# Attention, MoE and FFN in one kernel: the next expert's weights split by slices of 1024, in another order

## The chip, the cores and the metric

The kernel runs on one core of a Trainium2 chip. The metric is the device time of one execution in microseconds. TensorE (PE in the profile) multiplies matrices; its weight loads have a row of their own (PEld). VectorE (DVE), ScalarE (ACT) and GpSimd (POOL) compute elementwise. SyncE (SP) issues DMA transfers; POOL issues the indirect ones, which gather or scatter rows.

## What is computed

```python
attn_out = _attn_ref(**attn_kwargs)                 # 2 x 8 heads x 768 x 64, window 128, 4 sinks
x = np.ascontiguousarray(attn_out.transpose(0, 2, 1, 3)).reshape(B * S, H * D)   # 1536 x 512
x = _moe_ref(x=x, **moe_kwargs)                     # 8 experts, top 1
return _moe2_ref(x=x, **moe2_kwargs)                # (relu(x @ w_in) ** 2) @ w_out, d_ff 2048

# in _moe_ref, disp holds each expert's tokens (at most 384)
h = np.maximum(np.einsum('ecd,edf->ecf', disp, w1), 0.0)    # w1: 512 x 1024 for each expert
y = np.einsum('ecf,efd->ecd', h, w2)                        # w2: 1024 x 512 for each expert
out[i] = gate_w[i] * y[expert_idx[i], pos[i]]
```

## The kernel before

The kernel has three stages: attention with routing, the experts (MoE), and the last FFN. The change lies in the MoE stage.

**Precision.** Every fp32 matrix product is made of three matmuls on a high and a low part: `a_h b_h + a_h b_l + a_l b_h`. A tile is split by two instructions: ScalarE copies it to `h` in the type fp32r, and VectorE subtracts `h` from it into `l`. The weights of an expert are 4 MB, eight slices of 128x1024: four of `w1`, four of `w2`. `Weights.split` (L141) splits half a slice, 512 columns, at a time, so an expert has 16 such splits, each with a copy on ScalarE (L144) and a subtraction on VectorE (L145).

**Raw weights.** `fetch` (L135) loads a slice from memory into a ring of six raw slots. `freed` (L119) is called when a slice's second half is split; it lets `pull` issue the next load, which goes on SP's queue and waits for VectorE's subtraction of the slice that held the slot, six slices back.

**Order of the work.** The order of each engine's instructions is that of the Python code (a manual schedule). For expert `e` the loop calls `body(e, 0, ...)` for its first block of 128 tokens, then `more` for further blocks; these are behind an `If` on the expert's count, read at run time, so after the first block every engine passes a conditional branch and, later, the place where its two ways join. `body` splits the weights of expert `e + 1` between its own steps, and the table `HEAVY` says how many splits go into each gap. The steps are:

- `g1(0)`: 12 matmuls for the first half of h; then a gap, `relu(0)` (ScalarE, `hs`), `g1(1, [0, 1])`, a gap;
- `tr(0)`: TensorE transposes the first half of `hs`, ScalarE casts it to `hTh` (L913), VectorE subtracts into `hTl` (L914); `g1(1, [2, 3])`, a gap, `relu(1)`;
- `g2([0, 1])`: 6 matmuls into y; a gap, `tr(1)`, `g2([2, 3])`;
- point 2: `pre` transposes x for the same expert's second block (`xT1`) and the next expert's first (`xT0`); ScalarE casts them (L872), VectorE subtracts (L873) and computes the gates (L877, L878);
- a gap, `g2([4, 5])`, `g2([6, 7])`, a gap;
- `ys` (L956): VectorE scales y out of PSUM; POOL scatters it to `yd` (L957); then the splits that are left.

Each engine takes its queue in order, so a step behind a split waits for it. The last expert, 7, has no next one; it stages pieces of the FFN's weights (`piece_stage`, L174 to L189) instead, by the table `LAST`. At the end of its first block `load_y` (L1001) has SP load rows of `yd` (L1009), which waits for the scatters of the experts before, and TensorE transposes them to `x2T` (L1015).

Of the kernel before, what the change touches and what calls it, by code (L numbers as in the profile page):

```python
# [8 lines left out]
F32 = mybir.dt.float32  # L9
# [9 lines left out]
NOBODY = 8192  # L19
NWARM0 = 10  # L20

HEAVY = (3, 1, 2, 2, 0, 4)
LIGHT = (1, 1, 1, 1, 1, 1)
LAST = (0, 0, 1, 0, 1, 1)
NWARM = 2
PTACT = (0, 2)
SPOOL = ()
SDVE = ()
FILL = {0: 4, 1: 4, 2: 2, 3: 2}


# [1 line left out]
def kernel(  # L33
# [15 lines left out]
    nc = tc.nc  # L49
# [36 lines left out]
    def ps(tag, name):  # L86
        banks[tag].append(banks[tag].pop(0))
        return psum.tile([P, 512], F32, tag=f"b{banks[tag][-1]}", name=name)
# [18 lines left out]
    def pull(n):  # L107

        nonlocal held
        while n and stream and held + stream[0][0] <= NRAW:  # L110
            held += stream[0][0]
            n -= 1
            stream.pop(0)[1]()

    def freed(n=1):
        nonlocal held
        held -= n
        if eager:
            pull(NRAW)  # L119

    class Weights:
# [19 lines left out]
        def split(self, n, eng=None, hi=None):  # L141
            i, sl = n // 2, slice(n % 2 * 512, n % 2 * 512 + 512)
            t = self.raw[i]
            (hi or nc.scalar.copy)(self.h[i][:, sl], t[:, sl])  # L144
            (eng or nc.vector).tensor_sub(self.l[i][:, sl], t[:, sl], self.h[i].bitcast(F32)[:, sl])  # L145
            if n % 2:
                freed()

# [68 lines left out]
    W = {0: Weights(0, wx, "x"), 1: Weights(1, None, "y")}  # L219
# [629 lines left out]
    def gate_at(e, b):  # L849
        return gate[2 + b % 2 if b else e % 2]  # L850

    def load_x(e, b):
        if e >= E or b >= nblk:
            return
        nc.gpsimd.indirect_dma_start(
            out=x_at(e, b), out_offset=None, in_=xd[:, :], in_offset=bass.IndirectOffsetOnAxis(ap=src[:, b, e : e + 1], axis=0),
            bounds_check=NTOK - 1, oob_is_err=False,
        )

    def pre(e, b):  # L860
        if e >= E or b >= nblk:
            return
        p_ = ps("bg", "xT")
        for c in range(KD):
            nc.tensor.transpose(p_[:, c * P : (c + 1) * P], x_at(e, b)[:, c * P : (c + 1) * P], ident)
        pre_split(e, b, p_)
        pre_gate(e, b, x_at(e, b)[:, DM:])
# [12 lines left out]
    def body(e, b, splits, plan, also):  # L880
        xh, xl = xT[e, b]
        wts = W[e]
        splits = list(splits)

        def sp(n):
            for _ in range(n):
                if splits:
                    splits.pop(0)()

        hs = mp.tile([P, F], F32, tag="hs", name="hs", bufs=1)  # L890
        hp = [None, None]

        def g1(half, ks):
            if ks[0] == 0:
                hp[half] = ps("s" if half or b else "iv", "h")
            for kk in ks:
                r = slice(half * 512, half * 512 + 512)
                for m, (a, bb) in enumerate(((xh, wts.h), (xh, wts.l), (xl, wts.h))):
                    nc.tensor.matmul(hp[half], a[:, kk, :], bb[kk][:, r], start=(kk == 0 and m == 0), stop=(kk == KD - 1 and m == 2))

        def relu(half):
            nc.scalar.activation(hs[:, half * 512 : half * 512 + 512], hp[half], AF.Relu)

        hT = [None, None]

        def tr(half):
            p_ = ps("pt", "hT")
            for c in range(4):
                o0 = half * 512 + c * P
                nc.tensor.transpose(p_[:, c * P : (c + 1) * P], hs[:, o0 : o0 + P], ident)  # L910
            h_ = mp.tile([P, 512], F32R, tag="hTh", name="hTh", bufs=2)
            l_ = mp.tile([P, 512], F32R, tag="hTl", name="hTl", bufs=2)
            nc.scalar.copy(h_, p_)  # L913
            nc.vector.tensor_sub(l_, p_, h_.bitcast(F32))  # L914
            hT[half] = (h_, l_)

        y = ps("ot", "y")

        def g2(fs):
            for f in fs:  # L920
                h_, l_ = (x[:, (f % 4) * P : (f % 4 + 1) * P] for x in hT[f // 4])
                wh, wl = wts.h[KD + f // 2], wts.l[KD + f // 2]
                r = slice((f % 2) * 512, (f % 2) * 512 + 512)
                for m, (a, bb) in enumerate(((h_, wh), (h_, wl), (l_, wh))):
                    nc.tensor.matmul(y, a, bb[:, r], start=(f == 0 and m == 0), stop=(f == NF - 1 and m == 2))

        def point(i):
            for f in also.get(i, ()):
                f()

        plan = iter(plan)
        g1(0, [0, 1, 2, 3])
        sp(next(plan))
        relu(0)
        g1(1, [0, 1])
        sp(next(plan))
        tr(0)
        g1(1, [2, 3])
        sp(next(plan))
        relu(1)  # L940
        point(0)
        g2([0, 1])
        sp(next(plan))
        tr(1)
        point(1)
        g2([2, 3])
        point(2)
        sp(next(plan))
        g2([4, 5])
        point(3)  # L950
        g2([6, 7])
        point(4)
        sp(next(plan))
        y_ = mp.tile([P, DM + 1], F32, tag="ys", name="ys", bufs=2)
        nc.gpsimd.tensor_copy(y_.bitcast(I32)[:, DM:], src[:, b, e : e + 1])
        nc.vector.tensor_scalar(y_[:, :DM], y, gate_at(e, b), None, op0=ALU.mult)  # L956
        nc.gpsimd.indirect_dma_start(  # L957
            out=yd[:, :], out_offset=bass.IndirectOffsetOnAxis(ap=dst[:, b, e : e + 1], axis=0), in_=y_, in_offset=None,
            bounds_check=NTOK - 1, oob_is_err=False,
        )  # L960
        sp(len(splits))

    def more(e, b, also=()):

        if b >= nblk:
            for f in also:
                f()
            return
        with tc.If(vals[e] > b * P) as any_:  # L969
            if b + 1 >= XB:  # L970
                load_x(e, b + 1)
            body(e, b, [], LIGHT, {0: also, 3: [lambda: pre(e, b + 1)]})
            more(e, b + 1)
        if also:
            with any_.Else():
                for f in also:
                    f()
# [9 lines left out]
    stream += [(2, lambda p_=p_: piece_load(p_)) for p_ in order]  # L987
    eager = True
    pull(NRAW)

    def split_at(g, i):
        W[g].split(i, nc.gpsimd if i in SPOOL else None, nc.vector.tensor_copy if i in SDVE else None)


    CH = 512
# [6 lines left out]
    def load_y(c, tags):  # L1002

        c0, w = chunks[c]

        def ld(t):
            if t < w // P:
                r0 = c0 + t * P
                nc.sync.dma_start(yts[t % len(yts)], yd[r0 : r0 + P, :])  # L1009

        def go(t):
            yt = yts[t % len(yts)]
            p_ = ps(tags[t % 2], "x2T")
            for kk in range(KD):
                nc.tensor.transpose(p_[:, kk * P : (kk + 1) * P], yt[:, kk * P : (kk + 1) * P], ident)  # L1015
            n = c0 // P + t
            nc.gpsimd.tensor_copy(tok[:, n : n + 1], yt.bitcast(I32)[:, DM:])
            pv = p_.rearrange("p (k n) -> p k n", k=KD)
            hv, lv = (x[:, :, t * P : (t + 1) * P] for x in x2T[c])
            nc.scalar.copy(hv, pv)  # L1020
            nc.vector.tensor_sub(lv, pv, hv.bitcast(F32))  # L1021
            ld(t + len(yts))

        for t in range(len(yts)):
            ld(t)
        return [lambda t=t: go(t) for t in range(w // P)]
# [26 lines left out]
    for e in range(E):  # L1053
        g = e + 1
        if e > 0:
            W[g].alloc()
        for b in range(1, XB):
            load_x(e + 1, b)
        if g < E:
            splits = [(lambda i=i, g=g: split_at(g, i)) for i in range(16)]  # L1060
        else:
            splits = [ticks.tick] * (NPRE + 1)
            its = load_y(0, ("bg", "bg"))
        if nblk:
            also = {2: [lambda: pre(e, 1), lambda: pre(e + 1, 0), lambda: load_x(e + 2, 0)]}
            also[4] = its[:-1]
            body(e, 0, splits, HEAVY if g < E else LAST, also)
            if nblk > 1:
                vals[e] = nc.values_load(cnt[0:1, e : e + 1], min_val=0, max_val=cap)
            more(e, 1, its[-1:])  # L1070
        else:
            for f in splits + its:
                f()
# [197 lines left out]
```

## Time and profile before

| | us |
|---|---|
| median of 3 runs | 607.14 (607.09 to 607.84) |
| the profiled execution | 608.54 |
| its span, first to last instruction | 606.8 |
| TensorE busy | 575.8 (95%) |
| VectorE, ScalarE, GpSimd busy | 354.9, 297.2, 136.5 |

The profile is of one execution. A group's "mean" is the time from an instruction's start to its acknowledged end; in a row of like instructions the next starts before that end, so the pace is shorter. In square brackets stands the time that an engine was idle before an instruction, and what released it. A row of a table of stretches has the stretch and its length, then for PE, PEld, DVE, ACT and POOL the busy time and the number of instructions, then TensorE's granted clock as a share of full speed, the busy share of the 16 DMA engines, and GB/s.

### The profile page before, as it was taken

The page shows a single profiled execution, that of the slowest core. Times are in us where ns is not written, and L with a number is a line of the kernel's source. Part 1 is how long each engine was busy: PE and PEld are TensorE (multiplying, and loading weights), DVE is VectorE, ACT ScalarE, POOL GpSimd, SP SyncE. Part 2 cuts the span into 40 slices and gives each one's busy share as a digit, 9 for nine tenths or more (in the row PEclk, how much of TensorE's full clock was granted, in tenths as well). Part 3 has the DMA queues.
Part 4 walks back from the last instruction along what each step waited for, and adds up shares of the span by engine and source line. Part 5 has one row for each costly group of instructions (what it writes and reads, how often), then busy time and mean ns, then how long its engine had stood idle before and what let it go on. Part 6 is the DMA issues. An engine that isn't in the chain of part 4 may idle for free. (4 is left out here: it accounts for less than half of the span.)

```text
span 606.8 us, 9356 instructions
## 1 busy us (share of the span) xinstructions
PE 575.8 (95%) x3243; PEld 458.7 (76%) x3243; DVE 354.9 (58%) x838; ACT 297.2 (49%) x649; POOL 136.5 (22%) x235
## 2 busy tenths in 40 slices
PE   8999999979999999999899899999999999999994
PEld 4777778758887787777687677777888888888883
DVE  3788888747449966957752798996322322322222
ACT  4788878636248756746532455544222221322221
POOL 8544455233223413422211000000200000200002
PEclk9999999989999999999999899999999999999998
DMA  8698996446527985856731946441100000100001
GB/s 186 166 217 162 213 202 150 139 120 196 173 49 241 346 308 151 298 181 215 241 104 57 357 166 199 157 139 52 59 11 1 17 1 0 59 15 2 0 1 60
DMA packets 74625, 82.09 MB, mean 135 GB/s; under 512 B 42200, under 2 KB 53464, under 8 KB 74560
## 3 DMA queue, kind: packets, MB, share of 16 engines
q1 hardware_dynamic: 70608, 72.45, 41.6%
q0 software_dynamic: 3952, 8.82, 4.2%
q8 instruction: 35, 0.57, 0.4%
q14 instruction: 30, 0.25, 0.1%
HBM read 69.29 MB, written 16.08 MB: 141 GB/s over the span
## 5 line engine op out<-in xcount | busy, mean ns | idle before, releaser
L1113 DVE TENSOR_TENSOR xb<-xb 128x512 f32<-128x512 f32 (+1 forms) x48 | 31.6, 658 | 104.6 <-ACT xb L1112 104.6
L1112 ACT ACTIVATE xb<-a 128x512 f32<-128x512 f32 (+1 forms) x48 | 27.6, 575 | 113.8 <-PE a L1110 113.7
L1169 PE MATMUL out<-yl,gh 128*128 128x512 f32 (+1 forms) x188 | 75.8, 403 | 4.1 <-DVE yl L188 4.1
L1169 PE MATMUL out<-yh,gh 128*128 128x512 f32 (+1 forms) x188 | 75.7, 402 | 1.9 <-ACT gh L1128 1.9
L1169 PE MATMUL out<-yh,gl 128*128 128x512 f32 x173 | 68.8, 398 | 0.0
L1128 ACT CAST gh<-xb 128x512 fp32r<-128x512 f32 (+1 forms) x47 | 28.0, 597 | 64.1 <-DVE xb L1113 60.6
L454 ACT ACTIVATE p<-p,nm 128x260 f32<-128x260 f32 (+2 forms) x96 | 46.9, 489 | 17.3 <-DVE nm L442 16.2
L957 POOL DMA_INDIRECT yd<-ys,dst x14 | 26.0, 1857 | 118.7 <-DVE xl L145 33.3
L1130 DVE TENSOR_TENSOR gl<-xb,gh 128x512 fp32r<-128x512 f32 (+1 forms) x47 | 30.7, 653 | 33.8 <-ACT gh L1128 32.5
L1136 POOL DMA_INDIRECT out_dram<-raw,tok x12 | 11.8, 984 | 169.2 <-issue 69.5
L1110 PE MATMUL a<-x2Al,xh 128*128 128x512 f32 (+1 forms) x128 | 47.9, 374 | 0.6 <-DVEq L1078 0.6
L1110 PE MATMUL a<-x2Ah,xh 128*128 128x512 f32 (+1 forms) x128 | 48.2, 376 | 0.3 <-PEq L1078 0.3
L1110 PE MATMUL a<-x2Ah,xl 128*128 128x512 f32 (+1 forms) x128 | 47.8, 374 | 0.0
L1169 PEld LDWEIGHTS out<-yl,gh 128*128 128x128 f32 (+1 forms) x188 | 34.9, 186 | 14.5 <-DVE yl L188 6.2
L145 DVE TENSOR_TENSOR yl<-raw,yh 128x512 fp32r<-128x512 f32 x64 | 40.4, 686 | 5.8 <-ACT yh L144 5.7
L1169 PEld LDWEIGHTS out<-yh,gh 128*128 128x128 f32 (+1 forms) x188 | 34.8, 185 | 10.9 <-ACT gh L1128 2.4
L1169 PEld LDWEIGHTS out<-yh,gl 128*128 128x128 f32 x173 | 32.9, 190 | 8.1 <-DVE gl L1130 0.4
L144 ACT CAST xh<-raw 128x512 fp32r<-128x512 f32 x64 | 36.2, 619 | 1.1 <-DMA raw<-in_moe_w_dram 0.8
L144 ACT CAST yh<-raw 128x512 fp32r<-128x512 f32 x64 | 35.5, 623 | 2.2 <-PEq L969 1.7
L914 DVE TENSOR_TENSOR hTl<-hT,hTh 128x512 fp32r<-128x512 f32 x28 | 19.3, 690 | 28.4 <-ACT hTh L913 28.4
L145 DVE TENSOR_TENSOR xl<-raw,xh 128x512 fp32r<-128x512 f32 x48 | 30.2, 687 | 1.9 <-ACT xh L144 1.6
L529 PE MATMUL ot<-pts,v 128*64 128x128 f32 x352 | 30.1, 286 | 0.5 <-ACT pts L496 0.5
(224 smaller groups left out, 1407.8 us busy)
## 6 DMA issues: line engine op xcount, KB each, us to landing
raw<-in_moe_w_dram SPq DMA_DIRECT2D x64, 512.0 KB, 4.6
raw<-in_moe_w_in_dram SPq DMA_DIRECT2D x16, 512.0 KB, 4.8
raw<-in_moe_w_out_dram SPq DMA_DIRECT2D x8, 1024.0 KB, 5.3
yd<-zero SPq DMA_DIRECT2D x12, 256.5 KB, 6.3
xd<-x SPq DMA_DIRECT2D x12, 256.5 KB, 5.0
xb<-yd SPq DMA_DIRECT2D x12, 256.5 KB, 4.4
kr<-in_k_dram SPq DMA_DIRECT2D x12, 256.0 KB, 5.7
qr<-in_q_dram SPq DMA_DIRECT2D x12, 256.0 KB, 6.2
```

The lines of the kernel that those rows point to most:

```text
L144: (hi or nc.scalar.copy)(self.h[i][:, sl], t[:, sl])
L145: (eng or nc.vector).tensor_sub(self.l[i][:, sl], t[:, sl], self.h[i].bitcast(F32)[:, sl])
L454: nc.scalar.activation(d["p"][:, h, :width], d["p"][:, h, :width], AF.Exp, bias=d["nm"][:, h : h + 1], scale=-1.0, accum_out=d["sm"][:, h ...
L529: nc.tensor.matmul(d["o"][i * D : (i + 1) * D, c * P : (c + 1) * P], vt[b, kb][:, h, :], t_, start=i not in d["started"], stop=False, skip ...
L914: nc.vector.tensor_sub(l_, p_, h_.bitcast(F32))
L957: nc.gpsimd.indirect_dma_start(out=yd[:, :], out_offset=bass.IndirectOffsetOnAxis(ap=dst[:, b, e : e + 1], axis=0), in_=y_, in_offset=None ...
L1110: nc.tensor.matmul(a_[:, :w], a, bb[:, kk, :w], start=(kk == 0 and m == 0), stop=(kk == KD - 1 and m == 2))
L1112: nc.scalar.activation(r_, a_[:, :w], AF.Relu)
L1113: nc.vector.tensor_mul(r_, r_, r_)
L1128: nc.scalar.copy(gh[:, :w], r_)
L1130: nc.vector.tensor_sub(gl[:, : w - k_], r_[:, : w - k_], gh.bitcast(F32)[:, : w - k_])
L1169: nc.tensor.matmul(o, a, bb[:, r], start=(f == 0 and m == 0), stop=(f == NFF - 1 and m == len(prods) - 1))
```

## The change

The weights of the next expert are split by whole slices: `split_slice` does 128x1024 in one copy and one subtraction, so an expert has 8 splits instead of 16. `body` has one gap more, behind `tr(1)`, and the tables have seven entries. In halves of a slice the gaps held 3, 1, 2, 2, (none behind `tr(1)`), 0, 4, with 4 left behind `ys`; now they hold 2, 0, 1, 1, 1, 1, 2 whole slices, that is 4, 0, 2, 2, 2, 2, 4 halves, and none is left. `LAST` gets an entry of 0 for the new gap. Two empty settings (`SPOOL`, `SDVE`) go.

```diff
-HEAVY = (3, 1, 2, 2, 0, 4)
-LIGHT = (1, 1, 1, 1, 1, 1)
-LAST = (0, 0, 1, 0, 1, 1)
+HEAVY = (2, 0, 1, 1, 1, 1, 2)
+LIGHT = (0, 0, 0, 0, 0, 0, 0)
+LAST = (0, 0, 1, 0, 0, 1, 1)
...
+        def split_slice(self, i):
+            nc.scalar.copy(self.h[i], self.raw[i])
+            nc.vector.tensor_sub(self.l[i], self.raw[i], self.h[i].bitcast(F32))
+            freed()
...
         g2([0, 1])
         sp(next(plan))
         tr(1)
+        sp(next(plan))
         point(1)
         g2([2, 3])
...
-            splits = [(lambda i=i, g=g: split_at(g, i)) for i in range(16)]
+            splits = [(lambda i=i, g=g: W[g].split_slice(i)) for i in range(8)]
```

ScalarE, the start of expert 1's first block, before (`xh` are the high parts of expert 2's weights):

```order
L144 CAST xh_2854<-raw_76 128x512 x2
L144 CAST xh_2856<-raw_76 128x512
L902 ACTIVATE hs<-h 128x512
L144 CAST xh_2856<-raw_76 128x512
L913 CAST hTh<-hT 128x512
L144 CAST xh_2858<-raw_74 128x512 x2
```

and with the change:

```order
L148 CAST xh_2838<-raw_76 128x1024
L148 CAST xh_2840<-raw_76 128x1024
L905 ACTIVATE hs<-h 128x512
L916 CAST hTh<-hT 128x512
L148 CAST xh_2842<-raw_74 128x1024
```

The half that stood behind the first `hs` now stands ahead of it.

ScalarE, the end of the same block, before:

```order
L144 CAST xh_2860<-raw_74 128x512 x2
L913 CAST hTh<-hT 128x512
L872 CAST xT1h<-xT 128x512
L872 CAST xT0h<-xT 128x512
L144 CAST xh_2862<-raw_75 128x512 x2
L144 CAST xh_2864<-raw_75 128x512 x2
L144 CAST xh_2866<-raw_76 128x512 x2
L144 CAST xh_2868<-raw_76 128x512 x2
L1069 TENSOR_LOAD cnt
```

and with the change:

```order
L148 CAST xh_2844<-raw_74 128x1024
L916 CAST hTh<-hT 128x512
L148 CAST xh_2846<-raw_75 128x1024
L875 CAST xT1h<-xT 128x512
L875 CAST xT0h<-xT 128x512
L148 CAST xh_2848<-raw_75 128x1024
L148 CAST xh_2850<-raw_76 128x1024
L148 CAST xh_2852<-raw_76 128x1024
L1070 TENSOR_LOAD cnt
```

The fifth slice has moved ahead of `xT1h` and `xT0h`; three slices are left behind them instead of four.

VectorE at the same place (`xl` are the low parts), before:

```order
L873 TENSOR_TENSOR xT0l<-xT,xT0h 128x512
L877 TENSOR_SCALAR gate_2474<-xb_197 128x1
L878 RECIPROCAL gate_2474<-gate_2474 128x1
L145 TENSOR_TENSOR xl_2863<-raw_75,xh_2862 128x512 x2
L145 TENSOR_TENSOR xl_2865<-raw_75,xh_2864 128x512 x2
L956 TENSOR_SCALAR ys<-y,gate_2475 128x512
L145 TENSOR_TENSOR xl_2867<-raw_76,xh_2866 128x512 x2
L145 TENSOR_TENSOR xl_2869<-raw_76,xh_2868 128x512 x2
L1069 TENSOR_LOAD cnt
```

and with the change:

```order
L876 TENSOR_TENSOR xT0l<-xT,xT0h 128x512
L880 TENSOR_SCALAR gate_2474<-xb_197 128x1
L881 RECIPROCAL gate_2474<-gate_2474 128x1
L149 TENSOR_TENSOR xl_2849<-raw_75,xh_2848 128x1024
L149 TENSOR_TENSOR xl_2851<-raw_76,xh_2850 128x1024
L149 TENSOR_TENSOR xl_2853<-raw_76,xh_2852 128x1024
L960 TENSOR_SCALAR ys<-y,gate_2475 128x512
L1070 TENSOR_LOAD cnt
```

`ys` stood behind two slices of four; now it stands behind three and is the last of the block. TensorE, POOL and SP issue the same instructions in the same order as before.

## Rows read from the trace of the kernel before

**Rows 1.** Table of stretches: the turns of experts 1 and 2.

```profile
174.70:188.10 13.40, 13.25 (x67) 10.57 (x65) 9.79 (x19) 8.21 (x16) 4.57 (x5) 1.00 0.59 180
188.10:203.10 15.00, 13.64 (x64) 10.36 (x65) 13.63 (x27) 11.80 (x23) 6.28 (x5) 1.00 0.85 275
```

**Rows 2.** Timeline of PE: start and duration in us; experts 2, 3, 7.

```profile
191.90 0.40 PE L899 MATMUL h<-xl,xT0h 128*128 128x512 f32 x1
192.13 0.40 PE L899 MATMUL h<-xh,xT0l 128*128 128x512 f32 x1
192.84 0.63 PE L910 MATMUL hT<-ident,hs 128*128 128x128 f32 x4 [0.30 <-ACT yh L144]
...
194.93 0.40 PE L925 MATMUL y<-xl,hTh 128*128 128x512 f32 x1
196.00 0.50 PE L925 MATMUL y<-xh,hTl 128*128 128x512 f32 x1 [0.67 <-DVE hTl L914]
...
208.55 0.66 PE L910 MATMUL hT<-ident,hs 128*128 128x128 f32 x4 [0.99 <-ACT hs L902]
...
289.46 0.63 PE L910 MATMUL hT<-ident,hs 128*128 128x128 f32 x4 [0.30 <-DVEq L969]
...
298.85 0.65 PE L1015 MATMUL x2T<-ident,xb 128*128 128x128 f32 x4 [0.86 <-DMA xb<-yd]
```

**Rows 3.** Timeline of ACT, from expert 1's second hTh to expert 2's first hs.

```profile
182.95 0.59 ACT L913 CAST hTh<-hT 128x512 fp32r<-128x512 f32 x1
184.74 0.59 ACT L872 CAST xT1h<-xT 128x512 fp32r<-128x512 f32 x1 [1.20 <-PE xT L865]
...
185.70 4.27 ACT L144 CAST xh<-raw 128x512 fp32r<-128x512 f32 x8
190.14 1.66 ACT L144 CAST yh<-raw 128x512 fp32r<-128x512 f32 x3 [0.17 <-ACTq L969]
191.71 0.59 ACT L902 ACTIVATE hs<-h 128x512 f32<-128x512 f32 x1
```

**Rows 4.** Timeline of DVE from expert 1's xT1l to expert 2's first hTl.

```profile
185.36 0.69 DVE L873 TENSOR_TENSOR xT1l<-xT,xT1h 128x512 fp32r<-128x512 f32 x1 [1.10 <-ACT xT1h L872]
...
187.07 2.50 DVE L145 TENSOR_TENSOR xl<-raw,xh 128x512 fp32r<-128x512 f32 x4
189.48 0.74 DVE L956 TENSOR_SCALAR ys<-y,gate 128x512 f32<-128x512 f32 x1
...
192.85 2.50 DVE L145 TENSOR_TENSOR yl<-raw,yh 128x512 fp32r<-128x512 f32 x4 [0.21 <-ACT yh L144]
195.26 0.68 DVE L914 TENSOR_TENSOR hTl<-hT,hTh 128x512 fp32r<-128x512 f32 x1
```

**Rows 5.** Groups of instructions, shapes apart: total busy us, mean ns of one | idle before.

```profile
L188 DVE TENSOR_TENSOR xl<-raw,xh 128x1024 fp32r<-128x1024 f32 x8 | 9.7, 1218 | 0.0
L186 ACT CAST xh<-raw 128x1024 fp32r<-128x1024 f32 x8 | 9.1, 1132 | 0.0
L144 ACT CAST xh<-raw 128x512 fp32r<-128x512 f32 x64 | 36.2, 619 | 1.1 <-DMA raw<-in_moe_w_dram 0.8 <-ACTq L969 0.2
```

**Rows 6.** ACT at expert 3's start; loads into raw; stretches (columns of rows 1).

```profile
206.11 1.89 ACT L144 CAST xh<-raw 128x512 fp32r<-128x512 f32 x3 [0.83 <-DMA raw<-in_moe_w_dram]
...
DMA to landing us min/median/max: 2.3/4.5/8.9
...
188.00:190.00 2.00, 1.90 (x8) 1.61 (x9) 2.00 (x4) 1.97 (x4) 0.00 (x0) 1.00 0.39 72
190.00:196.00 6.00, 5.03 (x23) 3.50 (x22) 5.79 (x11) 5.17 (x10) 4.38 (x3) 1.00 0.79 252
```

**Rows 7.** Timeline of POOL, two scatters; waits of SP's queue: total, times, longest.

```profile
287.63 2.54 POOL L957 DMA_INDIRECT yd<-ys,dst  x1 [10.20 <-issue]
...
164.61 1.00 POOL L957 DMA_INDIRECT yd<-ys,dst  x1 [8.39 <-DVE ys L956]
...
SPq L1009 <- DMA yd<-ys,dst: 5.6, 1, 5.6
```

More of the change, by code (lines that the diff above doesn't have):

```diff
@@ L20 @@
 NWARM0 = 10
-HEAVY = (3, 1, 2, 2, 0, 4)
-LIGHT = (1, 1, 1, 1, 1, 1)
-LAST = (0, 0, 1, 0, 1, 1)
+HEAVY = (2, 0, 1, 1, 1, 1, 2)
+LIGHT = (0, 0, 0, 0, 0, 0, 0)
+LAST = (0, 0, 1, 0, 0, 1, 1)
 NWARM = 2
 PTACT = (0, 2)
-SPOOL = ()
-SDVE = ()
 FILL = {0: 4, 1: 4, 2: 2, 3: 2}
@@ L989 @@
     pull(NRAW)
-    def split_at(g, i):
-        W[g].split(i, nc.gpsimd if i in SPOOL else None, nc.vector.tensor_copy if i in SDVE else None)
     CH = 512
```

## Prediction

> **What bounds the kernel now.** I read the trace in four steps. First a table of stretches, one for each expert's turn in the MoE stage, since only that stage is changed. Expert 1 (one block of tokens, 174.7 to 188.1) takes 13.4 us, of which TensorE is busy 13.25; expert 2, which issues the same matmuls, takes 15.0 [rows 1]. So the stage is bound by TensorE, except for 1.6 us of expert 2. Second, TensorE's own timeline shows where these go. Its matmuls start 0.23 us apart. In expert 2 the first transposes of hs start 0.71 after the last matmul, a loss of 0.48, and the first matmul that needs hTl starts 1.07 after the one before it, a loss of 0.84 [rows 2]. The same pair, equally long, stands in expert 5, and nowhere else: both experts follow one with a single block. Expert 3 follows such a one too; there the loss is one wait of 0.99 at the same transposes, for hs from ScalarE. Expert 7 loses 0.3 there (the release is VectorE's arrival at the join of the conditional block), and then waits 0.86 for x2T, for a DMA [rows 2].
>
> Third, ScalarE and VectorE before that place [rows 3, 4]. The eight half-slices that follow xT0h and xT0l keep ScalarE until 189.97 and VectorE until 192.64. Then come four halves of the next expert: hs starts at 191.71 and hTl at 195.26. So **a backlog of splits crosses from one expert into the next**. But both engines stand idle just ahead of that backlog: ScalarE 1.20 us before xT1h, VectorE 1.10 before xT1l. Into this hole the change puts a slice.
>
> **The change, part by part.**
>
> *Whole slices for halves.* In a run of eight halves ScalarE needs 0.52 each ((4.27 - 0.62) / 7, [rows 3, 5]), and VectorE 0.60 ((2.50 - 0.69) / 3, [rows 4]). No row has this split in one piece of 1024. The nearest are two lines of the FFN's staging that copy and subtract 128x1024 from the same tiles with a stride: 1.13 and 1.22 us, against 0.62 and 0.69 for the halves [rows 4, 5]. The upper end for a whole slice is that duration. The lower end adds to one half's pace the longer row's excess: 0.52 + 0.51 = 1.03 on ScalarE and 0.60 + 0.53 = 1.13 on VectorE. Instructions in a row overlap their ends, so I take 1.04 and 1.14. ScalarE then wins nothing over two halves, and VectorE 0.07 a slice, 0.5 us an expert, all of it beside TensorE's work.
>
> *The order, walked through at experts 1 and 2.* ScalarE: hTh ends its turn at 182.95 + 0.48 = 183.43 (two such casts take 0.96, from 184.74 to 185.70), the fifth slice at 184.47, and xT1h still starts at 184.74. Three slices follow xT0h instead of four: 185.70 + 3.12 = 188.82, and after the same 0.17 of branch [rows 3] the next expert's two slices end at 191.07. The last matmul that hs needs comes six before the one at 192.13, so it starts at 190.7 and is done 0.4 later: hs starts at about 191.2, 0.5 earlier than now, and ends at 191.8. TensorE wants it at 192.13 + 0.23 = 192.36. VectorE, idle since 184.26, has the fifth slice from ScalarE at 184.56 and ends it at 185.70, so xT1l is 0.34 late. TensorE reads it only with the next expert's third matmul; that has over a microsecond of room. The stretch from xT1l to the next slice takes 1.71 (185.36 to 187.07) and so ends at 187.41; three slices to 190.83; ys, now last, 0.66 to 191.49; the join 0.21 to 191.70 instead of 192.85; two slices to 193.98; hTl ends at 194.66. Without the first loss TensorE wants it at 194.93 + 0.23 - 0.48 = 194.68. **Both losses close: 1.32 less about 0.1 for the tie is 1.2 us.** Bounds: 0.97, the idle rows alone (0.30 + 0.67), and 1.6, the table's difference. Expert 5: again 1.2.
>
> *Expert 3.* Here ScalarE waited for raw weights: its first slice after 0.83 of idle at 206.11, and the run of three lasts 1.89 where it takes 1.66 elsewhere, so the second slice's data came at about 207.3 [rows 3, 6]. The loads are paced by VectorE, because a raw buffer is loaded again when its slice is subtracted, six slices on. The fifth slice of expert 1 is subtracted at 185.70 rather than 188.28, 2.6 us earlier, and its load falls into a stretch where the DMA moved 72 GB/s (share 0.39); after it the share is 0.79 up to 196 [rows 6]. Filling both holes is worth at most 2 x 0.61 + 6 x 0.21 = 2.5 us, so the data of that second slice comes between 204.8 and 207.3; I take 205.2, as the earliest load gains most. But hs now waits for the whole of it: 205.2 + 1.04 + 0.60 = 206.8. TensorE, 1.2 earlier, falls idle at 208.55 - 0.99 - 1.2 = 206.4. Left is a wait of 0.4 instead of 0.99: **0.6 gained**, between a loss of 1.5 (data no earlier) and a gain of 1.0.
>
> *Expert 7.* Losing the 0.3 at the join gains nothing, because x2T waits for a DMA anyway. That chain is: ys of expert 6, its scatter by GpSimd, the load of yd rows on SP's queue that waits 5.6 us for the scatter [rows 7], the transposes. ys moves behind three whole slices (3.42) and a fifth ahead of them, instead of four halves (2.41): 0.34 + 3.42 - 2.41 = 1.35 later. Against that, nothing follows ys on VectorE now. The scatter's instruction took 2.54 with four halves beside it and 1.00 with VectorE idle [rows 7]: 1.54 won back. I take nothing for the pair; bounds 1.35 lost and 0.3 gained. [...]
>
> POOL's queue otherwise keeps its order: scatters 1.4 later, x loads behind them, needed an expert later. SP's queue has the same loads in the same order. TensorE's instructions are unchanged.
>
> **Sum:** 1.2 + 1.2 + 0.6 = 3.0 us off. The profiled execution took 608.54, so 605.5 for such a one; it stands 1.4 above the median of 607.14, and I predict 607.1 - 3.0 = **604.1 us**, 603.3 to 604.9 with the bounds of the pairs and of expert 7.
>
> **Rivals.**
>
> *Expert 3 stays with the DMA.* The data comes near 206.3 or later, and the whole slice ahead of hs eats what is won: 2.4 minus 0.4 to 1.0, some 605.4. For it: ScalarE's 0.83, a landing of up to 8.9 us, and a share of 0.79 that is no hole [rows 6]. Against it: the stretch at 72 GB/s.
>
> *Coarse pieces cost what they save.* hs waits for the end of the second slice, ys for three. If a slice takes 0.2 more than I walked with, or starts late in the hole, ScalarE and VectorE enter expert 2 about 1 us later: the pair keeps about 1.0 of its 1.3, expert 3 loses 0.4, expert 7 loses 0.7. Net 607.1 - 0.6 + 1.1 = 607.6, no change. Against it: the hole is 1.20 long and the slice 1.04 to 1.13. [...]
>
> *Slower: the fifth slice is not there.* ScalarE takes its queue in order, so if the raw data is late, xT1h and xT0h stand behind it, and the next expert cannot start. Place: expert 2 and expert 5, whose fifth slice is loaded after the previous expert's seventh subtraction, about 189.7 in the walk, and wanted at about 196.9. That is 7.2 us, plus 1.4 of room up to xT0l. It decides from a landing of 8.6 us on; the median is 4.5 and the longest 8.9 [rows 6]. Two microseconds beyond would cost 2 at the start of the next expert and about 1 at its hs, in both: 607.1 - 3.0 + 6.0 = 610.1.
>
> *The change does nothing.* If the losses come from the joins themselves and not from the backlog, they stay: 607.1. Against it: expert 1, which comes after one with three blocks, runs without them [rows 1].
>
> **Chances.** Forecast 0.53; expert 3 with the DMA 0.23; coarse pieces 0.12; slower 0.05; nothing 0.07. A measurement of this kernel tells about 0.2%, 1.2 us, from no change. The first two are faster, with a small part of the third: 0.78. No change: most of the third and the last, 0.16. Slower: 0.06. The range takes the first two with their bounds and the near side of the third, 602.9 to 606.4.
>
> **What would show it.** Right: in experts 2 and 5 no idle of TensorE before the transposes of hs and before the first matmul with hTl; expert 2's turn 13.8 us instead of 15.0; ScalarE's 1.20 before xT1h filled; ys 1.35 later in its turn; scatters near 1 us in expert 6. Wrong: a DMA wait of ScalarE in front of the fifth slice, hs of expert 3 later against its matmuls than now, x2T of expert 7 waiting over 2 us, or whole slices of more than 1.2 us.

## Result, and the profile after the change

| | before | after |
|---|---|---|
| median | 607.54 (6 runs, 607.09 to 609.78) | 601.89 (6 runs, 600.45 to 603.93) |
| the profiled execution | 608.54 | 602.04 |
| its span | 606.8 | 600.3 |

The ratio is 0.9904, with a 95% interval of 0.9881 to 0.9927: 5.65 us less, where 3.0 were forecast. The spans differ by 6.5 us, and these can be laid out along the program. From the first matmul of expert 1 to the first matmul of the FFN it was 152.83 us and is 149.06: 3.8 less. From there to the FFN's third `a` it was 13.4 and is 9.4: 4.0 less. (`a` is the FFN's first product, with w_in, and `out` its second, with w_out; the third `a` stands behind the first `out`.) The rest has grown from 265.7 to 267.0. The prediction spoke of the first stretch alone.

**The MoE stage.** The same table of stretches as [rows 1], of after: experts 1, 2, 3 and 7, the last two with TensorE's columns alone.

```profile
174.80:188.10 13.30, 13.15 (x66) 10.47 (x64) 10.28 (x15) 8.46 (x12) 4.98 (x5) 1.00 0.62 199
188.10:201.90 13.80, 13.38 (x64) 10.48 (x65) 13.13 (x18) 11.05 (x15) 5.08 (x5) 1.00 0.92 319
...
201.90:228.30 26.40, 25.90 (x124) 1.00 0.78 274
...
281.40:323.90 42.50, 39.88 (x192) 1.00 0.42 141
```

Expert 2 takes 13.8 us instead of 15.0. Expert 3 took 27.3 and takes 26.4, expert 7 took 43.0 and takes 42.5; expert 5 went from 27.6 to 26.3. Now TensorE's timeline of after, at the places of [rows 2]:

```profile
192.14 0.39 PE L902 MATMUL h<-xh,xT0l 128*128 128x512 f32 x1
192.37 0.60 PE L913 MATMUL hT<-ident,hs 128*128 128x128 f32 x4
...
194.43 0.40 PE L928 MATMUL y<-xl,hTh 128*128 128x512 f32 x1
194.75 0.50 PE L928 MATMUL y<-xh,hTl 128*128 128x512 f32 x1
...
295.00 0.65 PE L1016 MATMUL x2T<-ident,xb 128*128 128x128 f32 x4 [0.81 <-DMA xb<-yd]
```

The transposes of hs start 0.23 us after the last matmul (it was 0.71), the first matmul with hTl 0.32 after the one before it (1.07). No wait stands at either. The wait for x2T in expert 7 is still there. ScalarE, where [rows 3] showed the hole and the backlog:

```profile
183.43 1.05 ACT L148 CAST xh<-raw 128x1024 fp32r<-128x1024 f32 x1
184.74 0.59 ACT L875 CAST xT1h<-xT 128x512 fp32r<-128x512 f32 x1 [0.26 <-PE xT L868]
...
185.70 2.95 ACT L148 CAST xh<-raw 128x1024 fp32r<-128x1024 f32 x3
189.10 2.00 ACT L148 CAST yh<-raw 128x1024 fp32r<-128x1024 f32 x2 [0.45 <-ACTq L973]
191.23 0.60 ACT L905 ACTIVATE hs<-h 128x512 f32<-128x512 f32 x1
...
202.77 1.05 ACT L148 CAST xh<-raw 128x1024 fp32r<-128x1024 f32 x1 [0.26 <-DMA raw<-in_moe_w_dram]
204.84 1.05 ACT L148 CAST xh<-raw 128x1024 fp32r<-128x1024 f32 x1 [1.02 <-DMA raw<-in_moe_w_dram]
205.80 0.59 ACT L905 ACTIVATE hs<-h 128x512 f32<-128x512 f32 x1
```

The fifth slice lies in the hole, and 0.26 us of it are left. In expert 3 ScalarE still waits for raw weights, 0.26 and 1.02 us, but hs ends at 206.39. VectorE, against [rows 4]:

```profile
184.51 1.23 DVE L149 TENSOR_TENSOR xl<-raw,xh 128x1024 fp32r<-128x1024 f32 x1
...
187.36 3.50 DVE L149 TENSOR_TENSOR xl<-raw,xh 128x1024 fp32r<-128x1024 f32 x3
190.77 0.74 DVE L960 TENSOR_SCALAR ys<-y,gate 128x512 f32<-128x512 f32 x1
191.73 2.37 DVE L149 TENSOR_TENSOR yl<-raw,yh 128x1024 fp32r<-128x1024 f32 x2 [0.21 <-DVEq L973]
194.01 0.68 DVE L917 TENSOR_TENSOR hTl<-hT,hTh 128x512 fp32r<-128x512 f32 x1
```

**The FFN's entry.** Here is what the prediction did not look at. When the last block of expert 7 ends, VectorE writes the last ys, POOL scatters it to yd, and all engines pass a join. Behind it VectorE has one subtraction left, of the last staged piece of the FFN's weights (`ticks.close()`); it frees the piece's raw slot, and SP's next loads of weights wait for that. ScalarE's first `gh` (the high part of the FFN's squared hidden values) in turn needs the scatter to have landed: it comes from a pool that is opened where the MoE's, with ys in it, was closed. The timelines of VectorE, POOL, SP, ScalarE and TensorE in this place, before:

```profile
327.46 0.75 DVE L956 TENSOR_SCALAR ys<-y,gate 128x512 f32<-128x512 f32 x1 [2.91 <-PEq L1078]
328.80 1.23 DVE L188 TENSOR_TENSOR yl<-raw,yh 128x1024 fp32r<-128x1024 f32 x1 [0.58 <-DVEq L1078]
...
328.97 1.92 POOL L957 DMA_INDIRECT yd<-ys,dst  x1 [10.78 <-DVEq L1078]
...
330.05 0.93 SPq L164 DMA_DIRECT2D raw<-in_moe_w_in_dram  x2
...
335.68 0.62 ACT L1128 CAST gh<-xb 128x512 fp32r<-128x512 f32 x1 [3.44 <-DMA yd<-ys,dst]
...
336.35 0.50 PE L1169 MATMUL out<-yh,gh 128*128 128x512 f32 x1 [1.94 <-ACT gh L1128]
...
338.22 0.63 PE L1169 MATMUL out<-yh,gl 128*128 128x512 f32 x1
338.65 0.63 PE L1169 MATMUL out<-yh,gh 128*128 128x512 f32 x1
```

And after:

```profile
323.70 0.75 DVE L960 TENSOR_SCALAR ys<-y,gate 128x512 f32<-128x512 f32 x1 [2.92 <-PEq L1079]
325.41 1.23 DVE L191 TENSOR_TENSOR yl<-raw,yh 128x1024 fp32r<-128x1024 f32 x1 [0.96 <-DVEq L1079]
...
325.20 0.98 POOL L961 DMA_INDIRECT yd<-ys,dst  x1 [10.78 <-DVEq L1079]
...
326.66 0.99 SPq L167 DMA_DIRECT2D raw<-in_moe_w_in_dram  x2
...
329.27 0.62 ACT L1129 CAST gh<-xb 128x512 fp32r<-128x512 f32 x1 [0.80 <-DVE xb L1114]
```

Before, the subtraction starts 0.58 us after ys and 0.17 ahead of the scatter; the scatter's instruction takes 1.92 us and ends 0.84 behind the issue of SP's first loads, which go out as the subtraction ends. The first gh of the FFN then waits 3.44 us for the scatter's DMA, and TensorE 1.94 for gh. After, the subtraction starts 0.96 after ys, 0.21 behind the scatter; the scatter takes 0.98, ends 0.48 ahead of SP's loads, and gh waits for nothing but its own input. TensorE's clock differs too. Two stretches of before and after, with the columns of [rows 1]:

```profile
335.00:341.00 6.00, 4.65 (x12) 3.40 (x13) 4.35 (x5) 2.30 (x4) 0.00 (x0) 0.72 1.08 380
```

```profile
331.00:337.00 6.00, 6.00 (x27) 4.84 (x26) 5.17 (x7) 2.98 (x4) 0.00 (x0) 1.00 1.09 381
```

Behind the idle time, matmuls start 0.43 us apart (338.22 to 338.65), against 0.23 in after's stretch (331.42 to 331.65); 12 instead of 27 matmuls fall into 6 us, of which 1.35 are the end of the wait. Of these 4.0 us 1.3 are given back in the rest. The likely place is the third `out`, since an FFN that begins earlier meets its own weights sooner: after waits twice there for the staging of `w_out`, before once and shorter (its row comes first).

```profile
350.10 0.50 PE L1169 MATMUL out<-yl,gh 128*128 128x512 f32 x1 [0.24 <-DVE yl L188]
...
342.27 0.50 PE L1170 MATMUL out<-yh,gh 128*128 128x512 f32 x1 [0.43 <-ACT yh L189]
343.70 0.51 PE L1170 MATMUL out<-yl,gh 128*128 128x512 f32 x1 [0.93 <-DVE yl L191]
```

So there were two questions for experiments. Does the gain of the experts come from the order, or from whole slices? And is the entry's gain the change's doing at all?

### The profile page after: what moved, and what is told of

Its sections match the earlier page's. It is cut to its first block, busy times and chain, and to the rows that moved or that the text cites. A ratio compares the mean times of both kernels' runs of the same rounds, so it can differ in the third digit from the quotient of the medians.

```text
span 600.3 us, 9242 instructions
## 1 busy us (share of the span) xinstructions
PE 572.4 (95%) x3241; PEld 457.8 (76%) x3243; DVE 351.2 (58%) x782; ACT 291.7 (49%) x593; POOL 131.1 (22%) x235
## 5 line engine op out<-in xcount | busy, mean ns | idle before, releaser
L961 POOL DMA_INDIRECT yd<-ys,dst x14 | 17.5, 1252 | 123.4 <-DVE ys L960 43.3
L149 DVE TENSOR_TENSOR yl<-raw,yh 128x1024 fp32r<-128x1024 f32 x32 | 38.1, 1222 | 2.8 <-ACT yh L148 2.1
L148 ACT CAST yh<-raw 128x1024 fp32r<-128x1024 f32 x32 | 32.5, 1053 | 2.4 <-PEq L973 1.7
L905 ACT ACTIVATE hs<-h 128x512 f32<-128x512 f32 x28 | 16.7, 598 | 32.0 <-PE h L902 29.5
L916 ACT CAST hTh<-hT 128x512 fp32r<-128x512 f32 x28 | 16.4, 587 | 27.4 <-PE hT L913 24.0
```

The lines of the kernel that those rows point to most:

```text
L148: nc.scalar.copy(self.h[i], self.raw[i])
L149: nc.vector.tensor_sub(self.l[i], self.raw[i], self.h[i].bitcast(F32))
L961: nc.gpsimd.indirect_dma_start(out=yd[:, :], out_offset=bass.IndirectOffsetOnAxis(ap=dst[:, b, e : e + 1], axis=0), in_=y_, in_offset=None ...
```

## Experiments

Kernels of one round share their runs of the kernel before. Where a single execution is quoted, 2 us up or down say little, because the clock at the start of expert 0 differs from one execution to the next. The same stretch of two executions of the unaltered kernel before, the one above and `b_again` below:

```profile
135.00:144.00 9.00, 8.63 (x31) 6.94 (x32) 6.35 (x23) 4.83 (x10) 6.56 (x7) 0.75 0.71 198
```

```profile
135.00:144.00 9.00, 9.00 (x43) 7.03 (x44) 8.05 (x26) 6.17 (x12) 6.89 (x7) 1.00 0.82 247
```

### First round: order or size of the pieces

**a_again**: the changed kernel, unaltered.

> The changed kernel again, unaltered. Two theories of the 5.6 us. (A) About 3.8 us is the MoE stage (the walk of the prediction) and about 2.5 us is the entry of the FFN, where the first gh waits for the last scatter of ys: that wait is gone because of the change. (B) The MoE stage gives 3.8 us in every run, and the wait at the FFN's entry is a draw that both kernels have in some runs. A: the wait is absent in this profile too, ratio 0.989 to 0.992. B: the wait may stand in this profile, with the granted clock at its lower level behind it, and the ratio may come out nearer 0.994.

601.37 us, ratio 0.9913 (0.9883 to 0.9943). VectorE's subtraction comes 0.96 us after ys again, behind a scatter of 0.99; the stretch from expert 1 to the FFN takes 149.3, experts 1 to 6 of it 106.5. Both parts repeat.

**halves_new_order**: the new order, with half-slices.

```diff
-HEAVY = (2, 0, 1, 1, 1, 1, 2)
+HEAVY = (4, 0, 2, 2, 2, 2, 4)
...
-            splits = [(lambda i=i, g=g: W[g].split_slice(i)) for i in range(8)]
+            splits = [(lambda i=i, g=g: W[g].split(i)) for i in range(16)]
```

> The new order with halves instead of whole slices: gaps of 4, 0, 2, 2, 2, 2, 4 halves. My theory (the order closes the backlog, whole slices only shorten it): two halves cost VectorE 0.07 and ScalarE 0.09 us more than a whole slice, six slices between the end of expert 1's xT0 and hTl of expert 2, so hTl of experts 2 and 5 comes about 0.4 us late again: 0.8 us of the MoE stage's 3.8 lost, 3.0 kept. Rival (the instruction count is what matters, fewer and longer ones): most of the gain goes, below 1.5 us kept in the MoE stage.

605.89 us, ratio 0.9953 (0.9934 to 0.9972). Experts 1 to 6 take 106.5 us, after's 106.5; before they took 109.9. So the order alone gives the gain of experts 1 to 6, and halves are as good there: the 0.8 us that I expected halves to lose did not show. Expert 7 takes 44.4 here, against 42.5 in after; more of that below. And the entry is as it was before (timelines of VectorE, POOL and ScalarE):

```profile
326.59 1.23 DVE L191 TENSOR_TENSOR yl<-raw,yh 128x1024 fp32r<-128x1024 f32 x1 [0.58 <-DVEq L1079]
...
326.76 1.91 POOL L961 DMA_INDIRECT yd<-ys,dst  x1 [10.78 <-DVEq L1079]
...
333.85 0.62 ACT L1129 CAST gh<-xb 128x512 fp32r<-128x512 f32 x1 [3.82 <-DMA yd<-ys,dst]
```

**whole_old_order**: whole slices, in about the old order; no slice in the hole, two left behind ys.

```diff
-HEAVY = (2, 0, 1, 1, 1, 1, 2)
+HEAVY = (2, 0, 1, 1, 0, 0, 2)
```

> Whole slices in the old order as nearly as whole slices allow: gaps of 2, 0, 1, 1, 0, 0, 2 slices, and two left behind ys. The backlog crosses into the next expert as before, only 0.6 us shorter on VectorE and 0.7 on ScalarE. My theory: the two losses in experts 2 and 5 shrink from 1.3 to about 0.8 each, expert 3 stays with its wait for raw data; 1.0 to 1.5 us gained in the MoE stage. Rival (instruction count): 3 us or more gained. The wait at the FFN's entry by A or B.

604.4 us, ratio 0.9941 (0.9925 to 0.9957). Experts 1 to 6 take 108.6, so most of the order's gain is gone; TensorE waits for hTl again, in expert 2 and, for 0.30 at 210.09, in expert 3. Expert 2:

```profile
195.73 0.50 PE L928 MATMUL y<-xh,hTl 128*128 128x512 f32 x1 [0.49 <-DVE hTl L917]
```

At the entry the idle time is 0.96, the scatter takes 0.98, and gh does not wait. The entry's gain went with the whole slices, whatever the order.

**ys_earlier**: one slice left behind ys.

```diff
-HEAVY = (2, 0, 1, 1, 1, 1, 2)
+HEAVY = (2, 0, 1, 1, 1, 1, 1)
```

> The change with one whole slice left behind ys (gaps of 2, 0, 1, 1, 1, 1, 1, one left). ys comes 1.1 us earlier in its turn, and a subtraction runs on VectorE beside the scatter. My theory: experts 2, 3 and 5 as in the changed kernel; the scatters of experts 1, 2, 4, 6 take about 2.5 us again instead of 1.0 to 1.6; expert 6's scatter is issued 1.1 us earlier and takes 1 to 1.5 longer, so x2T of expert 7 comes within 0.4 us of the changed kernel. Total within 0.5 us of it. Rival (the free VectorE behind ys is what counts): x2T of expert 7 over 1 us later.

601.74 us, ratio 0.9888 (0.987 to 0.9906). x2T starts 13.2 us after expert 7 does, against 13.6 in after, but its waits add to about the same. The scatters of experts 1, 2, 4 and 6 take 1.26 us with one subtraction beside them, not the 2.5 that I expected. The intervals of this and of a_again overlap: whether it is better is not shown.

### Second round: the subtraction and the last scatter

**b_again**: the kernel before, unaltered; one execution.

> The kernel before, again. (A) and (B) as for the changed kernel's repeat. A: the first gh waits for the last scatter as in the first profile (3.4 us of ScalarE's idle, 1.9 of TensorE's), and the MoE stage ends at 327.7 after the span's start within 0.5 us. B: the wait may be absent.

605.91 us. Idle time 0.58, scatter 1.91, gh waits 3.08: the entry repeats. The MoE stage ends at 325.5 and not within 0.5 us of 327.7; 2.1 of the 2.2 us lie ahead of expert 1.

**before_close_late**: the kernel before, with the last staged subtraction moved behind the FFN's first square, where it cannot meet the scatter.

```diff
-    ticks.close()
+    last_piece = ticks.open
+    piece_stage(last_piece, 2)
+    ticks.open = None
...
         nc.vector.tensor_mul(r_, r_, r_)
+        if (c, f) == (0, 0):
+            piece_stage(last_piece, 3)
```

> The kernel before, with one edit at the FFN's entry: VectorE's half of the last staged piece (its subtraction, 1.2 us) stands behind the first square of the FFN instead of ahead of it, so it cannot run beside the last scatter, and the load that it frees goes out behind the scatter. Theory (who is first at the entry, VectorE's subtraction or the scatter, decides whether the scatter lands in 4 or in 6.6 us): the wait of the first gh for the scatter is gone, TensorE keeps its clock, 2.0 to 3.0 us faster than before, scatter near 1.0 us. Rival (the scatter lands late for other reasons, the DMA's load): the wait stays, within 0.7 us of before.

606.1 us, ratio 0.9967 (0.9949 to 0.9984), 2.0 us less than before. POOL and ScalarE:

```profile
326.76 0.99 POOL L957 DMA_INDIRECT yd<-ys,dst  x1 [10.77 <-DVEq L1078]
...
330.83 0.62 ACT L1132 CAST gh<-xb 128x512 fp32r<-128x512 f32 x1 [0.81 <-DVE xb L1115]
```

Without the subtraction beside it the scatter takes 0.99, and gh does not wait for it. So closing the piece there is what costs, in the old order too. But the edit moves more than the subtraction. SP's loads that wait for it go out at 331.96, behind gh, and the 12 transfers that fill `out` with zeros, which follow the subtraction's loads on SP's queue in before, go out from 306.18. How much the scatter's slower instruction costs and how much the loads, the list of DMA issues tells, with the time from issue to landing: before (328 to 336), after_close_early (below; 322 to 335) and this run (326 to 334).

```profile
yd<-ys,dst POOLq DMA_INDIRECT x1, 6.6
...
yd<-ys,dst POOLq DMA_INDIRECT x1, 5.7
...
yd<-ys,dst POOLq DMA_INDIRECT x1, 3.3
```

In after_close_early the instruction takes only 1.24, but the loads go out 0.84 ahead of its end, as they do in before. From the instruction's end the scatter lands after 4.7, 4.5 and 2.3 us. So of the 3.3 us between before and this run 0.9 are the instruction, and some 2.4 come with the transfers that SP issues around its end.

**after_close_late**: the same edit on the changed kernel.

> The changed kernel with the late subtraction. Theory: the wait cannot come, so as the changed kernel in its runs without the wait, and better by the share of runs that have it; 0 to 1.0 us faster than the changed kernel, smaller spread. Rival: slower, as the raw slot is freed later and a load of the FFN's weights comes late.

602.4 us, ratio 0.9917 (0.9892 to 0.9943): as without the edit. There was nothing left to take away.

**after_close_early**: the changed kernel with `ticks.close()` ahead of the join.

```diff
+        WO.alloc()
+        ticks.close()
         head = nc.values_load(cnt[0:1, E : E + 1], min_val=0, max_val=NTOK)
...
-    WO.alloc()
-    ticks.close()
```

> The changed kernel, with the last staged piece closed ahead of the reading of the counts and the branch at the FFN's entry, so VectorE's subtraction starts about 1 us earlier and surely ahead of the last scatter. Theory as above: the wait of the first gh for the scatter is back, 2.0 to 3.0 us slower than the changed kernel, ratio 0.993 to 0.995 to the kernel before. Rival: no wait, ratio as for the changed kernel.

604.85 us, ratio 0.9952 (0.9934 to 0.997), so it costs. The scatter takes 1.24 us and does land late (5.7), but gh does not wait for it: gh's own input comes later still, since TensorE is late:

```profile
325.38 0.50 PE L1111 MATMUL a<-x2Al,xh 128*128 128x512 f32 x1 [1.32 <-DVEq L1081]
...
327.26 0.63 PE L1111 MATMUL a<-x2Al,xh 128*128 128x512 f32 x1
327.69 0.63 PE L1111 MATMUL a<-x2Ah,xl 128*128 128x512 f32 x1
```

VectorE comes to the join 0.7 us later (TensorE waits 1.32 for it, before and after 0.62 to 0.63), and then TensorE runs at the pace of 0.43 again: its granted clock is 0.84 from 323 to 328 and 0.82 from 328 to 333. An unplanned wait of a like price (0.9952 against the 0.9917 of after_close_late: 2.1 us) took the place of the one that was meant.

### Third round: why VectorE comes out earlier or later

Where the subtraction stands behind the join, kernels with half-slices have 838 instructions on VectorE in the whole program, and 0.58; those with whole ones have 782, and 0.96. The instructions between ys and the subtraction are the same.

**pad_dve8, pad_dve4, pad_act8**: the changed kernel with a tiny instruction behind each slice (56) on VectorE; behind every second (28); behind each, on ScalarE.

```diff
             nc.vector.tensor_sub(self.l[i], self.raw[i], self.h[i].bitcast(F32))
+            nc.vector.memset(pad, 0.0)
```

> VectorE again has the 838 instructions that it had before (56 tiny memsets of 128x1, one behind each slice), the slices stay whole and the order stays the change's. Theory A (the length of VectorE's instruction stream ahead of the join sets when it comes out of it): VectorE's idle time ahead of the last staged subtraction is 0.58 us again, the subtraction starts ahead of the last scatter, the scatter takes 1.9 us, the first gh waits over 3 us, and the time is about 604 us, ratio about 0.995. Theory B (the count does not matter, it is what the instructions are): 0.96 us, scatter about 1.0 us, no wait, 601.5 to 602.3 us, ratio about 0.991.

> 28 tiny memsets on VectorE, one behind every second slice. Theory A: VectorE's idle time at the join is neither bound to 0.58 nor to 0.96 us; whichever it is, the order of subtraction and scatter follows it (subtraction first and scatter near 1.9 us with under 0.76 us idle, scatter first and near 1.0 us with more). Theory B: 0.96 us.

> The same 56 tiny instructions on ScalarE instead of VectorE. Theory A: VectorE's idle time at the join stays 0.96 us, no wait for the scatter at gh, about 602 us. Rival (the whole program's length, or ScalarE's, sets it): 0.58 us and a wait of over 3 us at gh.

pad_dve8: 604.92 us, ratio 0.9942 (0.9925 to 0.9959). Its VectorE, POOL and ScalarE:

```profile
325.03 1.23 DVE L192 TENSOR_TENSOR yl<-raw,yh 128x1024 fp32r<-128x1024 f32 x1 [0.58 <-DVEq L1081]
...
325.21 1.91 POOL L963 DMA_INDIRECT yd<-ys,dst  x1 [10.70 <-DVEq L1081]
...
332.04 0.62 ACT L1131 CAST gh<-xb 128x512 fp32r<-128x512 f32 x1 [3.58 <-DMA yd<-ys,dst]
```

pad_dve4: 605.44 us, idle 0.58, scatter 1.91, gh waits 3.64. pad_act8: 600.82 us, idle 0.96, scatter 0.99, no wait. (The last two are single executions.) Theory A holds so far: whole slices gain at the entry because of how many instructions VectorE has ahead of it, not because of what these are. ScalarE's count has no part in it. (Fewer is not better as such: see the fourth round.)

**halves_close_late**: halves_new_order with the edit of before_close_late.

> The new order with half-slices, and the VectorE half of the last staged piece moved behind the first square of the feed-forward network, so that it cannot run into the last scatter. If the gain of the change is the order's gain plus the scatter that is no longer disturbed, these two edits together give what the change gives: no wait at gh, experts 1 to 6 in 106.5 us, 602 to 602.8 us, ratio about 0.991. If whole slices give something of their own beyond that, it stays at about 604 us, ratio 0.994 or more.

602.97 us, ratio 0.9912 (0.9888 to 0.9937); no wait at gh, scatter 0.98, experts 1 to 6 in 107.0. The new order and an undisturbed scatter give the change's whole gain with halves, within the intervals.

### Fourth round: the place in the stream

**start_8, start_28, start_128, start_256**: the changed kernel with so many memsets at the very start of the program, on VectorE.

```diff
+    for _ in range(28):
+        nc.vector.memset(pad, 0.0)
```

> 28 tiny memsets at the start of VectorE's stream, where it stands idle for some 6 us; all later instructions are the change's, 28 places further on. If the place in the stream decides: VectorE's idle time at the join 0.58 us, the last scatter near 1.9 us, a wait of over 3 us at the first gh, as with 28 memsets spread over the experts. If something else about those memsets did it: 0.96 us, scatter near 1.0 us, no wait.

> 256 memsets at the start, so every later instruction of VectorE moves by 256 places; the attention stage may start some 10 us late, which is not of interest here. [...]

> [...]

> 8 memsets at the start. No theory fixes the flip between 0 and 28 places: 0.96 us says that the change stands at least 8 places from it, 0.58 us that it stands nearer. Either way the scatter follows: near 1.0 us with 0.96, near 1.9 us with 0.58.

| memsets added | where | VectorE's instructions | idle at the join | last scatter |
|---|---|---|---|---|
| 0 | | 782 | 0.96 | 0.98 |
| 8 | start | 790 | 0.96 | 0.99 |
| 28 | start | 810 | 0.58 | 1.92 |
| 28 | experts | 810 | 0.58 | 1.91 |
| 56 | experts | 838 | 0.58 | 1.91 |
| 128 | start | 910 | 0.94 | 0.98 |
| 256 | start | 1038 | 0.94 | 0.99 |

It is the place: 28 memsets some 300 us earlier act like 28 in the experts. In every row the scatter follows the idle time. The times of these single executions tell nothing of it (604.98 with 8, no wait at gh; 602.37 with 28, gh waits 3.49): the granted clock at 135 to 144 was 0.62 with 8, and with 128 and 256 memsets expert 0's first matmul comes at 149.27 and 163.57, where it comes at 136.12 in after. Why some places cost 0.38 us more is open.

## Why the prediction was wrong

**The forecast part was right in kind and nearly in size.** In expert 2 the walk gave hs at 191.2, VectorE past the join at 191.70 and hTl done at 194.66; it was 191.23, 191.73 and 194.69, and the turn 13.8 us as forecast. Expert 5 gave 1.3 for 1.2. A whole slice costs ScalarE 1.05 us, 0.95 in a row of three ((2.95 - 1.05) / 2), where 1.04 was taken, and VectorE 1.23 and 1.14. So ScalarE does win something over two halves, but halves_new_order shows that nothing hung on it.

**Expert 3 was sized at 0.6 and gave 0.9.** The data of the second slice came at 204.84 instead of 205.2. The forecast's own arithmetic says why that is all of it: hs was wanted by 206.4, ended at 206.39, and the wait of 0.99 [rows 2] is gone.

**Expert 7 was sized at nothing, and what it gave is not settled.** In the profiled execution it gave 0.4, and the two sides were there. In expert 7's turn the scatter of expert 6 starts 1.3 us later (4.2 us after the turn's start; before 2.9) and takes 1.04 instead of 2.54 [rows 7]:

```profile
285.58 1.04 POOL L961 DMA_INDIRECT yd<-ys,dst  x1 [11.69 <-DVEq L973]
```

It ends 0.2 earlier, and x2T starts 13.6 us after expert 7 does, not 14.1. But in a_again x2T starts 14.6 after it, and the expert still takes 42.8 us. And in 10 of the 14 profiled executions with the new order (that of ys_earlier counted in) TensorE's granted clock falls to 0.84 or less around its waits for x2T, and the expert takes 43.4 to 45.3; in the other four it takes 42.4 to 42.8. With the old order (four executions) the clock stayed at 1.00 there, and it took 42.7 to 43.0. The same stretch of halves_new_order and of after, with TensorE's columns alone:

```profile
294.00:305.00 11.00, 8.68 (x37) 0.84 0.70 230
...
294.00:305.00 11.00, 8.67 (x46) 1.00 0.74 247
```

It is busy for the same time in both, with 37 matmuls in one and 46 in the other. So the gain of 0.4 is one draw, and most executions with the new order lose 0.4 to 2.4 us here. No run settles whether the order brings the lower clock about; the bounds of 1.35 lost and 0.3 gained knew nothing of the clock.

**The step that failed is the sum**, "1.2 + 1.2 + 0.6 = 3.0 us off". It ends with expert 7 and so puts the FFN's entry at nothing, on the ground that "TensorE's instructions are unchanged" and "POOL's queue otherwise keeps its order". Both are true, but the last scatter, 1.92 us long in the trace of before, stood beside a 128x1024 subtraction of VectorE, as the scatter in [rows 7] that I did count stood beside four of 128x512. I asked which scatters the change itself moves, and not which others were slow for the same reason and might come loose. The runs show 4.0 us less at that entry in the trace (13.4 to 9.4), and 2.0 in the time when the entry alone is mended (before_close_late). By the ratios the two parts are about 2.9 us for the order (halves_new_order, 0.9953) and 2.0 for the entry (before_close_late, 0.9967); together 4.9, where both edits give 5.4 (0.9912) and the change 5.3 to 5.8 (0.9913, 0.9904). The intervals are wide, 1.7 to 4.0 for the first part and 1.0 to 3.1 for the second. So the parts add up within them, and no more than that is shown.

No reading of the diff could have told that VectorE would now be 0.38 us later at that join. In this sense the entry's gain is luck: 28 memsets more take it away again. The wait was in the trace, though, and the range should have held its loss: 3.0 and a further 2.0 give 602.1, below the low end of 602.9. The inner range, 603.3 to 604.9, was also narrower than its own bounds: with expert 3 at its 0.6, the bounds of the pairs and of expert 7 give 603.0 (2 x 1.6 + 0.6 + 0.3 = 4.1 off) to 605.9 (2 x 0.97 + 0.6 - 1.35 = 1.2 off).

**The rivals.** *Expert 3 stays with the DMA* had the wait right (0.26 and 1.02 us for data) but not what it costs. *Coarse pieces cost what they save* fell: a slice takes 1.05 and 1.23, and halves in the same order are no better. *Slower* did not come: the fifth slice found its data in experts 2 and 5. *Nothing* fell: in a_again as in after, experts 1 to 6 take 3.4 us less.

## What to carry to other kernels

Where a backlog of background work crosses into the next unit, look for a hole just ahead of it and move a piece there; here that was worth 3.4 us in the six experts, some 2.9 in the time, and the size of the pieces nothing there. And go through all places where the same two engines meet, beyond the edited stage: here a scatter issued by GpSimd and a VectorE subtraction started within 0.21 us of each other, a race that 0.38 us on one side turned, and it decided 2 us and more. Look also at what the subtraction sets free: here the loads that went out with its end delayed the scatter's landing more than the subtraction itself did (some 2.4 us against 0.9). Such a race is better settled in the program, as before_close_late does, than left to the number of instructions ahead of it.

## What the runs showed of the hardware

- VectorE came out of the same join 0.58 us after its last instruction or 0.94 to 0.96, depending on how many instructions its stream held (810 and 838 in the whole program, against 782, 790, 910 and 1038). Why is open.
- The last scatter takes 1.91 to 1.92 us when VectorE's 128x1024 subtraction starts 0.17 ahead of it, 1.24 when it starts 0.84 ahead (after_close_early), and 0.98 to 0.99 when it starts 0.2 behind, though the two then overlap by 0.8. When the subtraction is first, the scatter ends 0.85 to 0.86 us after the subtraction's end (before, halves_new_order, after_close_early, pad_dve8, pad_dve4, start_28). The subtraction takes 1.22 to 1.23 either way: the one that comes first is not slowed (the scatter takes 0.99 in before_close_late with no subtraction beside it), and VectorE not in either case. Why the scatter is slower behind the subtraction no run shows.
- The same scatter lands 6.6, 6.2 and 5.7 us after its issue where SP's loads go out 0.84 us ahead of the instruction's end (before, b_again, after_close_early), and 3.3 and 3.2 where none do (before_close_late, after_close_late). Where they go out 0.48 behind its end, gh starts 4.1 us after the issue without waiting for it (after).
- A TensorE that stood idle for 1.3 to 2.3 us at the FFN's entry mostly came back at a lower granted clock (0.72 from 335 to 341 before, after 1.94 us; 0.82 from 328 to 333 in after_close_early, after 1.32; 0.66 from 333 to 338 in pad_dve8, after 2.10) or with matmuls 0.43 us apart (halves_new_order, after 2.31; start_28, after 2.00), but not always: in pad_dve4, after 2.15 us of idle, it was 1.00 from 333 to 338 as well.
